# A Fourier-mixing and snake-MLP kernel: relayouts of the first batch on VectorE, filter halves by DMA, weight scaling on GpSimd, and the short chunk moved to the border of two batches

## The chip, the cores and the metric

The kernel runs on one core of a Trainium2 chip. The metric is the device time of one execution in microseconds (us), taken over several executions. On this core one run costs about 815 us and repeated runs mostly agree within a few us, so differences under about 0.3% are read only from several rounds. A change counts as faster or slower from 2% on; everything less is "the same".

The engines are TensorE (PE in the profile; PEld is its weight load), VectorE (DVE), ScalarE (ACT), GpSimd (POOL) and SyncE (SP, which here only issues transfers; SPq is its sequencer).

## The reference, cut to what matters

```python
X = np.fft.rfft(x, axis=1)                 # x: 8 batches x 3008 x 256
y = np.fft.irfft(X * (filt_r + 1j * filt_i)[None], n=3008, axis=1)
h = y.reshape(24064, 256) @ w_in           # 256 -> 2048
g = h + np.sin(alpha * h) ** 2 / alpha
out = g @ w_out                            # 2048 -> 256
```

## The kernel before

The Fourier transform of 3008 = 47 x 64 points is done as matmuls with tables, in four stages for each batch: first (tile `pa`), forward (`pb`), a product with the filter (`p`), inverse (`pc`), last (`pd`, which gives `y`). Between first and forward, and again between inverse and last, data must move from one layout over the partitions to another. Before, that is a round trip through DRAM: a write to `d`, then a read with another address pattern (`t`).

```python
def first(self, i):
    ...
    if j == 3:
        nc.sync.dma_start(out=self.d1_rows[:, 8 * ch:8 * ch + 8, :], in_=self.t1)
def load_t2(self, g):                       # the way back, in the other layout
    for p in range(2):
        marks["t2", g] = eng.dma_start(out=self.t2[g][64 * p:64 * p + 64, :, :],
                                       in_=self.d1[a0:a0 + 6, :, :].rearrange("s n c -> n s c"))
```

A complex product needs the filter in both partition halves. For the first `FUSED = 2` batches each unit has two products and two inverse matmuls; from then on it is *fused*: the spectrum is swapped between the halves by a small DMA (`xs`), and two more VectorE instructions (`cross`) let one inverse matmul do.

```python
def dup_filter(g):                          # VectorE fills the other halves, with a sign
    for ins in (nc.vector.tensor_copy(out=f_t[0][64:128, gs, :], in_=f_t[0][0:64, gs, :]),
                nc.vector.tensor_scalar(out=f_t[1][0:64, gs, :], in0=f_t[1][64:128, gs, :],
                                        scalar1=-1.0, scalar2=None, op0=ALU.mult)):
        behind(ins, marks["prod", 3 * g - 2] if g else s1_dve)
...
def weights_out(i):                         # w_out / alpha, in steps 4 to 7
    for jb in range(4 * i, 4 * i + 4):
        nc.vector.tensor_scalar(out=w2[:, jb, :], in0=w_out32[:, jb, :], scalar1=rec_t[:, jb:jb + 1],
                                scalar2=-0.5, op0=ALU.mult, op1=ALU.mult)
```

The MLP runs over chunks of 512 tokens in eight steps each: two hidden tiles (matmul `ph`, a sine on ScalarE into `cos`, the snake on VectorE into `v`) and, for the chunk before, projection matmuls (`po`). The Fourier stages of the next batch are put between these steps by hand: `put(step, function, ...)`.

```python
chunks = [(pb, c0, min(512, 2 * S - c0)) for pb in range(B // 2) for c0 in range(0, 2 * S, 512)]
```

A pair of batches has 6016 tokens, eleven chunks of 512 and one of 384, which stands at the end.

## Time and profile before

The median is 815.4 us (815.29 to 816.07); the profiled execution took 814.22 us with a span of 812.3 us.

| Mark in the trace | us |
|---|---|
| first forward matmul | 27.03 |
| first hidden-layer matmul (`ph`) | 53.46 |
| first projection matmul (`po`) | 69.18 |
| from there to the end of the span | 743.1 |

Two marks cut such a kernel well. Up to the first `ph` it is a start-up chain of dependent steps; between the first `ph` and the first `po` it fills the first chunk; after that TensorE has work all the time. So "when does `po` start" and "how long is the rest" are two numbers to compare between versions.

The page's busy tenths in 40 slices (20.3 us each), before. The third row, PEclk, is the granted TensorE clock in tenths.

```profile
PE   5657999999999999999999999999999999999995
DVE  3669797789978998789987998779987999777772
PEclk9779999999999999999999999999999999999998
```

TensorE is loosely busy only in the first four slices. The windows view, before (length, then busy time and instruction count of each engine, granted clock, DMA share, GB/s):

```profile
90.00:180.00 90.00, 89.67 (x669) 62.35 (x667) 72.11 (x129) 71.95 (x142) 11.04 (x19) 1.00 0.59 144
180.00:300.00 120.00, 118.46 (x892) 82.36 (x890) 106.21 (x202) 97.67 (x196) 8.51 (x15) 1.00 0.60 135
300.00:800.00 500.00, 498.76 (x3716) 345.93 (x3714) 415.68 (x742) 391.58 (x770) 27.46 (x44) 1.00 0.47 113
```

From 90 us on TensorE (the first figure after the length) idles 3.1 us in 710. There is little to win there but fewer matmuls or those last microseconds. The timeline of TensorE, before (start, length, what ran; in brackets the idle time before it and what ended it):

```profile
27.03 1.01 PE L179 MATMUL pb<-t,d_t 128*128 128x256 f16 x4 [4.88 <-DMA t<-d]
...
51.38 0.81 PE L230 MATMUL pd<-wi_t,t 96*128 96x94 f16 x8 [8.56 <-DMA t<-d]
...
53.46 1.87 PE L368 MATMUL ph<-y,w 128*128 128x512 f16 x4 [0.17 <-ACT y L136]
...
69.18 1.04 PE L383 MATMUL po<-w,v 128*128 128x256 f16 x8
```

Both relayouts show as a wait for a DMA: 4.88 and 8.56 us. And the VectorE work that the change will touch, from VectorE's timeline before: a filter copy with a sign, and four scalings of `w_out`.

```profile
30.32 0.56 DVE L275 TENSOR_SCALAR filt<-filt 64x1536 f16<-64x1536 f16 x1
...
62.58 1.13 DVE L351 TENSOR_SCALAR w<-w_out,rec_t 128x256 f16<-128x256 f32 x4
```

Each scaling took 0.33 to 0.35 us.

### The profile page before, as it was taken

What the parts mean: (1) busy time and instruction counts of PE and PEld (TensorE: products, weight loads), DVE (VectorE), ACT (ScalarE), POOL (GpSimd) and SP (SyncE); (2) the same over time, 40 slices, a digit from 0 to 9 for tenths busy, and PEclk for the clock granted to TensorE, in tenths of its full rate; (3) what the DMA queues carried; (4) which work ended last, traced back from release to release, by engine and by line L of the source; (5) the groups of instructions that cost most, each with busy time, mean ns of one, the idle gap of its engine ahead of it and who ended that gap; (6) DMA issues with size and microseconds to landing.
All of it is one profiled execution on the core that took longest, in us unless ns stands there. A gap on an engine that the chain in (4) does not pass through costs nothing.

```text
span 812.3 us, 16130 instructions
## 1 busy us (share of the span) xinstructions
PE 771.4 (95%) x5649; PEld 527.5 (65%) x5649; DVE 652.4 (80%) x1191; ACT 612.8 (75%) x1200; POOL 65.4 (8%) x111
## 2 busy tenths in 40 slices
PE   5657999999999999999999999999999999999995
PEld 2324676676666776667667676667667676666674
DVE  3669797789978998789987998779987999777772
ACT  4547787788878888778887887778887887777662
POOL 3210300110020000200002000200002000000000
PEclk9779999999999999999999999999999999999998
DMA  9985755466576465644657554654558333411111
GB/s 213 227 260 132 186 113 148 127 137 141 117 185 149 97 144 126 184 95 95 140 159 178 111 104 116 193 127 104 115 139 214 73 91 84 116 37 40 40 40 46
DMA packets 86201, 104.44 MB, mean 129 GB/s; under 512 B 10388, under 2 KB 72868, under 8 KB 86120
## 3 DMA queue, kind: packets, MB, share of 16 engines
q1 hardware_dynamic: 73904, 73.45, 34.3%
q0 software_dynamic: 10288, 29.11, 18.0%
q10 hardware_dynamic: 1928, 0.86, 0.4%
q8 instruction: 44, 0.72, 0.4%
q14 instruction: 37, 0.30, 0.1%
HBM read 58.02 MB, written 49.81 MB: 133 GB/s over the span
## 4 chain that ended last, share of the span: by engine, by line
PE 88%; DMA 5%; DVE 2%; ACT 2%; issue 1%; POOL 0%; SPq 0%; ACTq 0%; DVEq 0%; POOLq 0%
PE po L383 39%; PE ph L368 38%; PE pa L159 4%; PE pc L210 3%; PE pb L179 3%; PE pd L230 2%; DMA t<-d 2%; DMA x<-in_x_dram 2%; DVE v L372 1%; ACT cos L371 1%; DMA d<-t 1%; ACT t L136 1%; DVE p L193 1%; DMA d<-g 0%; DVE t L138 0%
## 5 line engine op out<-in xcount | busy, mean ns | idle before, releaser
L372 DVE SCALAR_TENSOR_TENSOR v<-cos,ph 128x512 f16<-128x512 f32 (+1 forms) x768 | 483.5, 672 | 119.3 <-ACT cos L371 116.2
L371 ACT ACTIVATE cos<-ph 128x512 f32<-128x512 f32 (+1 forms) x768 | 411.5, 591 | 99.7 <-PE ph L368 98.9
L368 PE MATMUL ph<-y,w 128*128 128x512 f16 (+1 forms) x1536 | 388.5, 375 | 0.8 <-DVE y L138 0.6
L383 PE MATMUL po<-w,v 128*128 128x256 f16 x3008 | 389.0, 272 | 0.0
L383 PEld LDWEIGHTS <-v 128*128 128x128 f16 x3008 | 289.2, 98 | 77.7 <-issue 1.7
L368 PEld LDWEIGHTS <-w 128*128 128x128 f16 x1536 | 148.1, 98 | 104.3 <-issue 3.6
L182 ACT CAST xf<-pb 128x512 f16<-128x512 f32 x96 | 56.9, 594 | 20.4 <-PE pb L179 17.3
L389 ACT COPY o<-po 128x512 f32<-128x512 f32 x96 | 55.6, 579 | 17.9 <-PE po L383 16.3
L136 ACT CAST t<-pa 96x512 f16<-96x512 f32 x88 | 51.2, 585 | 22.8 <-PE pa L159 22.6
L159 PE MATMUL pa<-x,wf_t 94*96 94x512 f16 x128 | 51.0, 408 | 11.7 <-DMA x<-in_x_dram 8.3
L230 PEld LDWEIGHTS <-t 96*128 96x128 f16 x512 | 36.1, 99 | 34.3 <-DMA t<-d 11.0
L170 POOL DMA_DIRECT2D t<-d x56 | 37.0, 676 | 251.1 <-PE ph L368 183.6
L230 PE MATMUL pd<-wi_t,t 96*128 96x94 f16 x512 | 43.0, 208 | 11.5 <-DMA t<-d 10.1
L193 DVE TENSOR_TENSOR p<-xf,filt 128x512 f16<-128x512 f16 x120 | 47.8, 418 | 6.3 <-ACT xf L182 6.1
L136 ACT CAST y<-pd 128x376 f16<-128x376 f32 x82 | 39.3, 480 | 17.0 <-PE pd L230 16.6
L136 ACT CAST g<-pc 128x512 f16<-128x512 f32 x65 | 38.4, 590 | 11.8 <-PE pc L210 11.6
L210 PE MATMUL pc<-p,e_t 128*128 128x256 f16 x240 | 44.0, 278 | 2.7 <-DVE p L193 1.5
L179 PE MATMUL pb<-t,d_t 128*128 128x256 f16 x192 | 38.2, 282 | 5.9 <-DMA t<-d 4.9
L118 POOL DMA_DIRECT2D x<-in_x_dram x32 | 17.0, 536 | 262.8 <-PE pc L210 145.9
L138 DVE CAST t<-pa 96x512 f16<-96x512 f32 x40 | 27.2, 680 | 12.6 <-PE pa L159 12.6
L210 PEld LDWEIGHTS <-e_t 128*128 128x128 f16 x240 | 23.0, 99 | 16.2 <-issue 2.5
L200 DVE TENSOR_TENSOR p<-p,xs 128x512 f16<-128x512 f16 x72 | 30.6, 425 | 2.5
(31 smaller groups left out, 155.2 us busy)
## 6 DMA issues: line engine op xcount, KB each, us to landing
d<-t SPq DMA_DIRECT2D x32, 384.0 KB
d<-g SPq DMA_DIRECT2D x64, 192.0 KB
t<-d SPq DMA_DIRECT2D x32, 384.0 KB
x<-in_x_dram POOLq DMA_DIRECT2D x32, 376.0 KB, 6.2
t<-d POOLq DMA_DIRECT2D x56, 192.0 KB, 7.0
xs<-xf SPq DMA_DIRECT2D x144, 64.0 KB
out_dram<-o SPq DMA_DIRECT2D x72, 94.0 KB
w_in<-in_moe_w_in_dram POOLq DMA_DIRECT2D x2, 1024.0 KB, 8.9
```

What stands on the lines that cost most here:

```text
L136: marks["act"] = nc.scalar.copy(out=dst, in_=src)
L159: marks["pe"] = nc.tensor.matmul(out=ps[0:NK, :], lhsT=wf_t, rhs=self.x[ch][:, 2 * j:2 * j + 2, :], start=True, stop=True)
L179: nc.tensor.matmul(out=ps[:, i, :], lhsT=d_t[:, s, :], rhs=self.t2[s // 6][:, s % 6, :], start=True, stop=True)
L182: nc.scalar.copy(out=self.xf[u], in_=ps)
L193: marks["prod", u] = nc.vector.tensor_tensor(out=pt, in0=self.xf[u], in1=f_t[k][:, 2 * u:2 * u + 2, :], op=ALU.mult)
L210: nc.tensor.matmul(out=ps[:, i, :], lhsT=e_t[:, k, 2 * w + i, :], rhs=pt[:, i, :], start=(k == 0), stop=(k == len(pr) - 1))
L230: nc.tensor.matmul(out=psv[:, i, :], lhsT=self.t4[ch][:, 4 * half + i, cb * 128:cb * 128 + 128], rhs=wi_t, start=True, stop=True)
L368: nc.tensor.matmul(out=ps[:, 0:n], lhsT=w1[:, cb, jb * 128:jb * 128 + 128], rhs=y_cols[:, cb, c0:c0 + n], start=(cb == 0), stop=(cb == 1))
L371: nc.scalar.activation(out=cs[:, 0:n], in_=ps[:, 0:n], func=AFT.Sin, bias=float(np.pi / 2))
L372: marks["snake"] = nc.vector.scalar_tensor_tensor(out=v[k][:, jb, 0:n], in0=cs[:, 0:n], scalar=-1.0, in1=ps[:, 0:n], op0=ALU.add, op1=ALU. ...
L383: nc.tensor.matmul(out=pso[k][:, t % 2, :], lhsT=v[k][:, jb, 128 * t:128 * t + 128], rhs=w2[:, jb, :], start=(jb == 0), stop=(jb == 15))
L389: nc.scalar.copy(out=o[:, 0:nb, :], in_=pso[k][:, 0:nb, :])
```

## The change

The intent is to shorten the start-up chain. Batch 0 no longer goes through DRAM: VectorE transposes 32x32 blocks of 32-bit pairs in place of each round trip. The filter halves are copied by DMA, now without the sign, so batch 0 takes the sign from a second inverse table. GpSimd, which in the kernel before ran only four memsets of 0.1 us and the issue of transfers, scales `w_in` and half of `w_out`. Later batches need the negated filter half, so GpSimd flips its sign in place (`negate`), and batch 1 is fused like the rest (`FUSED = 1`). The 384-token chunk moves to the border of the two batches of a pair.

```diff
-FUSED = 2
+FUSED = 1
...
+    for g in range(2):                     # filter halves by DMA, no sign
+        for k in range(2):
+            gs = slice(12 * g, 12 * g + 12)
+            nc.gpsimd.dma_start(out=f_t[k][64 - 64 * k:128 - 64 * k, gs, :],
+                                in_=f_t[k][64 * k:64 * k + 64, gs, :])
...
+    def turn(dst, src):
+        nc.vector.transpose(out=dst.bitcast(UINT32).rearrange("p s c k -> p c (s k)"),
+                            in_=src.bitcast(UINT32).rearrange("p s c k -> p c (s k)"))
+    def turn_back(i):
+        hc, cs = i // 2, slice(32 * (i % 2), 32 * (i % 2) + 32)
+        turn(t4_0[hc][:, :, cs], g_0[hc][:, :, cs])
...
+    for i in range(4):
+        turn(t2_0[i // 2][:, :, 32 * (i % 2):32 * (i % 2) + 32], t1_0[:, :, 32 * i:32 * i + 32])
...
+        ins = nc.gpsimd.tensor_tensor(out=w1[:, :, js], in0=w32, in1=cos_cols[...], op=ALU.mult)
...
+    nc.vector.reciprocal(out=rec, in_=al)  # now just before the hidden layer
...
-            nc.vector.tensor_scalar(
+            (nc.gpsimd if jb in range(8, 16) else nc.vector).tensor_scalar(
                 out=w2[:, jb, :], in0=w_out32[:, jb, :], scalar1=rec_t[:, jb:jb + 1],
                 scalar2=-0.5, op0=ALU.mult, op1=ALU.mult)
...
-    chunks = [(pb, c0, min(512, 2 * S - c0)) for pb in range(B // 2) for c0 in range(0, 2 * S, 512)]
+    chunks = [(pb, c0, 384 if c0 == 2560 else 512) for pb in range(B // 2)
+              for c0 in [*range(0, 2561, 512), *range(2944, 2 * S, 512)]]
...
+    def negate(i):
+        gs = slice(6 * i, 6 * i + 6)
+        nc.gpsimd.tensor_scalar(out=f_t[1][0:64, gs, :], in0=f_t[1][0:64, gs, :],
+                                scalar1=-1.0, scalar2=None, op0=ALU.mult)
+    for i in range(4):
+        put(9, negate, i)
...
-        z = 48 * b - 2 * (b % 2)
+        z = 48 * b - 0 * (b % 2)
...
-            inv = 22.5 + u if b == 1 else ...
-            fwd = inv - (1.5 if b == 1 else 6)
+            inv = 23 + 1.3 * u if b == 1 else ...
+            fwd = inv - (5 if b == 1 else 6)
```

The cuts hold the new tables, eight filler matmuls before the hidden layer (`warm_pe`, meant for TensorE's clock), the order of the loads, and the block loop of batch 0 (twelve blocks of forward, product and inverse).

## The prediction

> **What bounds it now.** Two regimes. From 100 to 800 us the windows view gives TensorE 696.9 busy of 700 us: dense, so only fewer matmuls help there. Before that stands a start-up chain: the timeline has the first hidden-layer matmul at 53.46 us, and the chain of waits shows why. First-stage matmuls end at 16.9; the DRAM relayout follows (write 4.9 us, read back 4.3 us; first forward matmul at 27.0); products and inverse matmuls run to 43.4 (VectorE 9.7 of 10 us busy at 30-40, including filter copies of 0.57 and 0.56 us); then the second relayout (3.2 + 3.8 us) to 51.4. After it, the first chunk is VectorE-bound (13.8 of 15.7 us busy); the first projection matmul starts at 69.2. DMA is at or over 0.8 of its engines for most of the first 69 us.
>
> **Removed.** Both DRAM round trips of batch 0 (26.9-17.5 = 9.4 us, and 51.4-43.4 = 8 us), VectorE's eight filter copies (4.5 us), weight scaling on VectorE (4.9 us) and half of the 5.5 us of output-weight scaling. Batch 1 becomes fused: 24 matmuls fewer at 0.109 us = 2.6 us.
>
> **Added.** Eight block transposes of 1024 32-bit elements. [...] of which four stand on the chain in front and about two behind. Filters must be loaded whole and copied by DMA before the products: from the 205 to 270 GB/s of the first 20 us I estimate both halves of the filter landed at 19.5 us, the first copies at 23.5, the second at 29. So products wait for the copies[...]. ScalarE then evacuates both sides, 2 x 0.59 us per block of twelve. GpSimd scales w1[...].
>
> **Stages after the change (estimates).** Products from 23; inverse ends 37-38; two transposes; first hidden matmul at 41 (36 to 46) rather than 53.5. The first chunk takes VectorE 2.5 us less: first projection at 55-57 rather than 69.2, unless w_out (after alpha on a full DMA queue, estimated landing 45-54 us) holds VectorE. From there TensorE's work is dense and 2 us shorter. Batch 1, now three products per unit at one unit per 1.3 steps, loads VectorE 8.9, 10.3, 11.2 and 9.1 us in four consecutive half chunks in which TensorE has 8.5 to 8.7: I subtract 3 us for that. Sum: about -12.5 -2 +3, and a margin of 2 lost to weights or the clock's recovery: nearly all of it from the critical start-up chain. The 384-token chunk only moves a deadline.
>
> **Predicted: 802 us, 794 to 811 in 8 of 10 cases.** Faster by over 2% (below 799.1) 0.30; within 2% 0.68; slower 0.02.
>
> **What would show it.** First forward matmul near 19-20 us, first product near 23 and released by a filter-copy DMA; [...] first hidden matmul near 41; [...] TensorE idle 2-4 us more than before in the stretch of batch 1's products, released by VectorE; 24 fewer 256-column inverse matmuls per run in the dense part.
>
> **What would make it wrong.** Filter copies much faster or slower than 250 GB/s; strided transposes at twice my estimate; GpSimd's weights slowed by VectorE and pacing the first chunk (slower by up to 5 us); w_out late; or batch 1's VectorE load not costing TensorE anything (then near 798, just faster).

"My estimate" in the last paragraph is the time of a transpose. The time of two transposes is inside the 41 us, and so inside the 12.5 us; it is the author's estimate. The sum as written is 815.4 − 12.5 − 2 + 3 = 803.9 us, with the margin of 2 it is 805.9, and 802 was put down. "The clock's recovery" is about the granted clock, which in the kernel before was 0.60 from 20 to 30 us, 0.70 from 50 to 60 and 1.00 from 60 to 70.

## The result, and the profile after

The changed kernel took 823.3 us (median of 4 runs, 820.88 to 824.38) against 815.35 (4 runs, 815.29 to 816.07). The ratio is 1.009, with a 95% interval from 1.0067 to 1.0116: "the same" by the 2% rule, but above the predicted range of 794 to 811. Ratios here are the mean time of one kernel's fast runs over the mean of the other's fast runs of the same rounds, so they are not quite the ratio of the medians.

The profiled execution took 824.38 us, span 822.6 us. Busy tenths after:

```profile
PE   5774989999999999999999999999999999999995
DVE  6788669779987899789987899789987899777772
PEclk9976999999999999999999999999999999999999
```

The start is denser than before, but the fourth slice (62 to 82 us) has TensorE at 4 tenths and the clock at 6. TensorE's timeline, after:

```profile
20.30 1.06 PE L339 MATMUL pb<-t_h,d_t 128*128 128x128 f16 x8
...
45.18 6.26 PE L453 MATMUL ph<-y,w 128*128 128x512 f16 x16
...
73.53 1.87 PE L453 MATMUL ph<-y,w 128*128 128x512 f16 x4 [12.68 <-DVE v L457]
...
75.62 1.91 PE L468 MATMUL po<-w,v 128*128 128x256 f16 x8
```

The first hidden matmul is 8.3 us earlier than before, as intended. Then one hidden tile waits 12.68 us for a snake on VectorE, and the first projection comes 6.4 us *later* than before. VectorE's timeline, after, has the reason for the wait in its last lines:

```profile
14.19 3.63 DVE L310 STREAM_TRANSPOSE t_h<-t 128x1024 uint32<-128x1024 uint32 x2 [0.38 <-ACT t L149]
17.68 2.31 DVE L310 STREAM_TRANSPOSE t<-t 128x1024 uint32<-128x1024 uint32 x2
...
25.18 4.28 DVE L349 TENSOR_TENSOR p<-xf,filt 128x512 f16<-128x512 f16 x11 [1.30 <-DMA filt<-filt]
...
35.29 7.26 DVE L310 STREAM_TRANSPOSE t_h<-t_h 128x1024 uint32<-128x1024 uint32 x4
...
43.96 0.93 DVE L426 RECIPROCAL rec<-al 16x128 f32<-16x128 f32 x1
...
54.60 1.95 DVE L435 TENSOR_SCALAR w<-w_out,rec_t 128x256 f16<-128x256 f32 x4
...
58.12 14.77 DVE L435 TENSOR_SCALAR w<-w_out,rec_t 128x256 f16<-128x256 f32 x4
```

The same four scalings that took 1.13 us before take 14.77 us. VectorE counts as busy all that time, so a table of busy shares does not give it away; the length of the instruction does. The view of this one source line, after, gives the count and the shortest, median and longest of them in ns:

```profile
L435 DVE TENSOR_SCALAR w<-w_out,rec_t x8: 498/1546/4161, 54.6 to 68.7; 128x256 f16<-128x256 f32 x8
```

And GpSimd's timeline, after:

```profile
38.66 9.58 POOL L389 TENSOR_TENSOR w<-w_in,cos_all 128x768 f16<-128x768 f32 x6
52.65 3.75 POOL L435 TENSOR_SCALAR w<-w_out,rec_t 128x256 f16<-128x256 f32 x8 [4.42 <-DMA w_out<-in_moe_w_out_dram]
56.38 16.36 POOL L505 TENSOR_SCALAR filt<-filt 64x1536 f16<-64x1536 f16 x4
```

The longest scaling took 4.16 us, and beside it GpSimd ran four sign flips of 4.09 us each, from 56.38 to 72.74 us. VectorE's 14.77 us end at 72.89. One scaling per flip fits both: taken singly, the four took 2.53 us (it began while the first flip ran) and then 4.16 us three times. Also note the line at 54.60: these four scalings took 1.95 us instead of 1.13, and beside them GpSimd ran scalings of 0.47 us each.

Last, the windows after:

```profile
60.00:75.00 15.00, 1.85 (x5) 0.69 (x5) 15.00 (x8) 0.84 (x2) 12.74 (x4) 0.64 0.00 0
90.00:180.00 90.00, 83.89 (x610) 56.49 (x609) 70.83 (x135) 67.83 (x136) 13.12 (x21) 0.98 0.62 156
180.00:300.00 120.00, 119.87 (x901) 83.11 (x898) 105.17 (x194) 97.94 (x192) 8.24 (x14) 1.00 0.55 129
300.00:800.00 500.00, 499.89 (x3725) 346.37 (x3723) 421.28 (x756) 395.63 (x780) 27.73 (x46) 1.00 0.47 115
```

Three things are seen. From 60 to 75 us TensorE has 1.85 us of work and its clock falls to 0.64. From 90 to 180 us, the stage of batch 1, it idles 6.1 us, where before it idled 0.3. From 180 us on it is denser than before: 0.2 us idle in 620 after, 2.8 before.

So the span grew by 10.3 us as follows: first hidden matmul 8.3 us earlier, first chunk 14.7 us longer (30.4 instead of 15.7 us), the rest 3.9 us longer (747.0 instead of 743.1).

### Theories

*Lock.* The flips on GpSimd hold something that VectorE's scalings need, so each scaling waits out a whole flip. What that something is, no trace here shows. Its rival: the scalings wait for the late `w_out` or for the queue of work, and the flips only run beside them.

*Fused batch 1.* Fusing it costs more than its 24 saved matmuls give. Within it are two rivals for the cause: VectorE's three products per unit are too much (the prediction), or the swaps `xs` come late.

*Start-up* (S). What keeps the hidden layer at 45 instead of 41 us are the late reciprocal and the four last transposes standing one behind the other.

### The profile page after: what moved, and what is told of

The parts are those of the page before. It is cut to its first block, busy times and chain, and to the rows that moved or that the text cites. A ratio compares the mean times of both kernels' runs of the same rounds, so it can differ in the third digit from the quotient of the medians.

```text
span 822.6 us, 16328 instructions
## 1 busy us (share of the span) xinstructions
PE 774.6 (94%) x5745; PEld 530.3 (64%) x5745; DVE 672.1 (82%) x1184; ACT 616.1 (75%) x1203; POOL 89.9 (11%) x122
## 4 chain that ended last, share of the span: by engine, by line
PE 81%; DVE 8%; DMA 6%; ACT 2%; issue 1%; POOL 1%; ACTq 0%; POOLq 0%
PE po L468 37%; PE ph L453 36%; DVE v L457 3%; PE pa L170 3%; PE pd L247 2%; PE pb L190 2%; DVE w L435 2%; PE pc L221 2%; DMA xs<-xf 2%; DMA filt<-in_filt_i_dram 2%; DMA t<-d 1%; DVE t_h L310 1%; DMA filt<-filt 1%; ACT t_h L149 1%; DMA d<-t_h 1%
## 5 line engine op out<-in xcount | busy, mean ns | idle before, releaser
L457 DVE SCALAR_TENSOR_TENSOR v<-cos_all,ph 128x512 f16<-128x512 f32 (+1 forms) x768 | 483.0, 672 | 109.8 <-ACT cos_all L456 106.4
L456 ACT ACTIVATE cos_all<-ph 128x512 f32<-128x512 f32 (+1 forms) x768 | 411.4, 591 | 114.3 <-PE ph L453 111.7
L453 PE MATMUL ph<-y,w 128*128 128x512 f16 (+1 forms) x1536 | 390.7, 378 | 12.8 <-DVE v L457 12.7
L193 ACT CAST xf<-pb 128x512 f16<-128x512 f32 x84 | 49.9, 594 | 18.5 <-PE pb L190 13.8
L149 ACT CAST t_h<-pa 96x512 f16<-96x512 f32 x77 | 45.1, 586 | 10.9 <-PE pa L170 10.7
L247 PEld LDWEIGHTS <-t_h 96*128 96x128 f16 (+1 forms) x512 | 35.9, 98 | 26.9 <-DVE t_h L310 4.6
L247 PE MATMUL pd<-wi_t,t_h 96*128 96x94 f16 (+1 forms) x512 | 42.5, 206 | 4.6 <-DVE t_h L310 3.5
L170 PE MATMUL pa<-x,wf_t 94*96 94x512 f16 x112 | 43.0, 386 | 2.2 <-ACT t_h L149 2.1
L210 DVE TENSOR_TENSOR xs<-xs,filt 128x512 f16<-128x512 f16 x84 | 35.1, 418 | 6.1 <-DMA xs<-xf 6.0
L204 DVE TENSOR_TENSOR p<-xf,filt 128x512 f16<-128x512 f16 x84 | 35.1, 418 | 2.0 <-ACT xf L193 2.0
L221 PE MATMUL pc<-p,e_t 128*128 128x256 f16 x168 | 32.1, 273 | 3.7 <-ACT y L149 2.8
L151 DVE CAST y<-pd 128x376 f16<-128x376 f32 x49 | 26.6, 543 | 0.6 <-PE pd L247 0.6
```

The source lines that it names most:

```text
L149: marks["act"] = nc.scalar.copy(out=dst, in_=src)
L170: marks["pe"] = nc.tensor.matmul(out=ps[0:NK, :], lhsT=wf_t, rhs=self.x[ch][:, 2 * j:2 * j + 2, :], start=True, stop=True)
L193: nc.scalar.copy(out=self.xf[u], in_=ps)
L221: nc.tensor.matmul(out=ps[:, i, :], lhsT=e_t[:, 2 * w + i, :], rhs=pt[:, i, :], start=(k == 0), stop=(k == len(pr) - 1))
L247: nc.tensor.matmul(out=psv[:, i, :], lhsT=lhsT, rhs=wi_t if self.b else wi0_t, start=True, stop=True)
L453: nc.tensor.matmul(out=ps[:, 0:n], lhsT=w1[:, cb, jb * 128:jb * 128 + 128], rhs=y_cols[:, cb, c0:c0 + n], start=(cb == 0), stop=(cb == 1))
```

## The experiments

Eleven kernels ran in three calls, each call on one chip beside the kernel before (medians of before: 814.51, 814.81 and 814.76 us). Except for e3, all gave right results. By the 2% rule each of them is "the same" as the kernel before. The columns ph and po are the starts of the first hidden and first projection matmul in the run's profile, "rest" is the span less po.

| Run | us, median (range) | ratio to before [95%] | ph | po | rest |
|---|---|---|---|---|---|
| before | 815.4 | 1 | 53.46 | 69.18 | 743.1 |
| after | 823.3 | 1.0091 [1.0067, 1.0116] | 45.18 | 75.62 | 747.0 |
| e1 flips after the scalings | 809.52 (808.12–811.44) | 0.9935 [0.9909, 0.9961] | 45.27 | 60.62 | 745.8 |
| e2 scalings on ScalarE | 812.82 (812.60–813.56) | 0.9977 [0.9956, 0.9998] | 44.92 | 62.71 | 748.1 |
| e3 two flips of four | 817.18 (815.97–817.72) | 1.0025 [1.0006, 1.0045] | 45.81 | 69.12 | 746.7 |
| e4 batch 1 unfused | 817.00 (815.73–817.95) | 1.0024 [1.0003, 1.0045] | 46.35 | 61.07 | 753.6 |
| e5 the same, short distance | 803.10 (802.17–806.48) | 0.9846 [0.9820, 0.9872] | 47.73 | 64.63 | 740.1 |
| e6 e1, x of batch 2 later | 807.07 (804.30–807.64) | 0.9892 [0.9866, 0.9918] | 45.52 | 62.42 | 742.5 |
| e7 e1, start-up reordered | 809.72 (808.60–810.95) | 0.9932 [0.9909, 0.9954] | 46.15 | 62.14 | 745.4 |
| e8 e1, swaps from ScalarE | 815.68 (814.53–817.40) | 1.0006 [0.9982, 1.0030] | 45.65 | 62.51 | 753.1 |
| e9 e5, reciprocal early | 802.64 (802.44–805.27) | 0.9858 [0.9845, 0.9871] | 43.68 | 60.49 | 740.3 |
| e10 e5, chunks as before | 807.91 (806.64–811.04) | 0.9923 [0.9908, 0.9938] | 45.44 | 61.11 | 743.8 |
| e11 e5, filter copies on VectorE | 804.63 (803.23–805.04) | 0.9870 [0.9856, 0.9884] | 45.87 | 63.06 | 740.0 |

The profiled execution of e5 was the slowest of its four (806.48 us), with a clock of 0.71 from 45 to 60 us, so its ph and po are late; its rest is what to read. The clock in that stretch differs between the other profiles too: 1.00 in e1, e4, e7 and e9, 0.97 in e2, 0.77 to 0.89 in after, e3, e6, e8, e10 and e11. e6 has e1's start unchanged, yet its first chunk took 16.9 us against 15.4 at 0.78, so a difference of 1 to 2 us in po can be the clock's and not the edit's.

### e1: the flips wait for the scalings

Nothing is removed. The flips only get a dependency on VectorE's last scaling.

```diff
+            if jb == 7:
+                marks["w_out_dve"] = ins
...
+        after(ins, marks["w_out_dve"])     # on each of the four flips
```

> Edit: the four GpSimd sign flips of the filter wait for the last output-weight scaling on VectorE; nothing else changes. Theory L ([...] each VectorE scaling that reads and writes SBUF waits out one 4.1 us GpSimd flip, which started first): the four scalings take about 0.35-0.5 us each instead of 14.8 us together, TensorE's wait of 12.7 us in the first chunk goes, time about 810 (808-812). Rival D (VectorE waits for the output weights' DMA or is slow by itself): the scalings stay slow, time 821-824. Rival G (GpSimd is simply late and the whole start waits for it): the stall only moves to a later wait, time 818-824.

It took 809.5 us, 13.8 us less than the changed kernel. VectorE's timeline, e1:

```profile
53.66 1.82 DVE L435 TENSOR_SCALAR w<-w_out,rec_t 128x256 f16<-128x256 f32 x4
...
57.05 1.13 DVE L435 TENSOR_SCALAR w<-w_out,rec_t 128x256 f16<-128x256 f32 x4
```

GpSimd's timeline, e1:

```profile
58.27 16.27 POOL L507 TENSOR_SCALAR filt<-filt 64x1536 f16<-64x1536 f16 x4 [1.53 <-DVE w L435]
```

The four scalings are back at 1.13 us, and the 12.7 us wait is gone. The flips take their 4.07 us as before, so it was not VectorE that made them long. And while they ran, from 56 to 76 us, twenty snakes on VectorE averaged 0.679 us, against 0.683 for the same shape in the kernel before. The snake has one input in PSUM, and these instructions were not held at all. The scaling, which was held, has one source tile and goes from SBUF to SBUF. Why the one was held and the other not, the trace does not show.

### e2: the scalings on ScalarE

```diff
-            (nc.gpsimd if jb in range(8, 16) else nc.vector).tensor_scalar(...)
+            if jb in range(8, 16): nc.gpsimd.tensor_scalar(...)
+            else: nc.scalar.mul(w2[:, jb, :], w_out32[:, jb, :], rec_h[:, jb:jb + 1])
```

> Edit: the eight VectorE scalings of the output weights are done by ScalarE instead; the GpSimd sign flips stay where they are, at the same time. Theory L: [...] its scalings take about 0.3-0.4 us each beside the flips, and the flips keep about 4.1 us each; time 808-812. Rival D: the ScalarE scalings wait for the same DMA, so the stall stays, 820-824. Rival G: stall stays as well.

It took 812.8 us. The flips begin at 55.86 us, as early as in the changed kernel. ScalarE's last four scalings, from 56.01 on and beside a flip, took 1.74 us together; its first four, before any flip, 1.72. The 12.7 us wait is gone with the flips left where they were. It is 3.3 us slower than e1: ScalarE has 3.5 us more to do in the first chunk, which took 17.8 us against 15.4; that the one comes of the other was not tested, and the rest is 2.3 us longer, with a granted clock of 0.77 from 62.7 to 70 us. So data and timing of `w_out` were not to blame: on ScalarE the same scalings run beside the same flips.

### e3: two flips instead of four (a wrong result on purpose)

```diff
-    for i in range(4):
+    for i in range(2):
         put(9, negate, i)
```

> Edit: only two of the four GpSimd sign flips are issued (a wrong result on purpose: half of the filter keeps its sign for batches 1 to 7). Theory L: two of the last four VectorE scalings are blocked for about 4 us each, the other two take about 0.35 us; stall halves to about 6 us; time 815-818. Rivals D and G without a lock: D unchanged 821-824; G also 815-818, so this run alone only sizes the dose.

Half of the flipped half keeps the wrong sign, so the result is wrong (relative error 0.67). VectorE's timeline, e3:

```profile
57.90 8.49 DVE L435 TENSOR_SCALAR w<-w_out,rec_t 128x256 f16<-128x256 f32 x4
```

Half the flips give about half the loss: 8.49 us (the first of the flips began at 57.55), and 6.1 us off the time of the changed kernel. With e1 and e2 this shows that the flips hold up the scalings: the loss follows the number of flips, goes away if they come after, and goes away if the scalings are done elsewhere. Through what they hold them up, no run here shows.

### e4 and e5: batch 1 unfused

Batch 1 takes two products and two inverse matmuls again. For this the second table must outlive batch 0, so it is put into the half of `y` that batch 1 fills later, and the flips move to step 44, behind batch 1's products. e4 keeps the distances of the changed schedule, e5 takes those of the kernel before.

```diff
-FUSED = 1
+FUSED = 2
-    e1_0 = by_half(t4_h[1])
+    e1_v = [y[:, i, 1]...[:, 0:2048] for i in range(2)]      # e4 and e5
-        put(9, negate, i)
+        put(44, negate, i)                                  # after batch 1's last product
-            inv = 23 + 1.3 * u if b == 1 else ...
-            fwd = inv - (5 if b == 1 else 6)
+            inv = 22.5 + u if b == 1 else ...                # e5 only
+            fwd = inv - (1.5 if b == 1 else 6)               # e5 only
```

> Edit: batch 1 goes back to two products and two inverse matmuls (no swap by DMA), its second table kept in the half of y that is still empty; the sign flips move behind batch 1's products (step 44). So the stall of the first chunk goes too: compare with e1_negate_late. Theory F (the fused form costs batch 1 about 6 us of TensorE idle in 90-180 us, through late swaps on the busy DMA queue, for 2.6 us of matmuls saved): about 3-4 us below e1, so about 806-807. Rival (the idle comes from the late reads of the relayout and the next batch's x loads on the DMA queue, not from the swaps): equal to e1 or 2.6 us slower, 810-813.

e4 was badly made and tells nothing of fusing. With forward five steps ahead of inverse, the four buffers of `p` hold only two units of two products, and VectorE stands waiting: it was busy for 11.79 us from 90 to 110 us and 12.17 from 110 to 130, against 17.60 and 17.04 in e5. The time was 817.0 us, the rest at 753.6 us.

> The first unfused run left forward and inverse 5 steps apart, so its four product buffers held only two units and VectorE waited for them; this one takes the distances of the kernel before (inverse at 22.5 + u, forward 1.5 steps ahead). To compare with e1_negate_late (809.5). Theory F (the fused form of batch 1 costs TensorE about 6 us of idle through swaps that come late): TensorE's idle between 75 and 180 us falls from 6.9 to 1-3 us, 24 more matmuls cost 2.6 us, time 805-808. Rival (the idle is caused by the relayout reads and x loads alone): idle stays at 5-7 us, time 810-813.

e5 took 803.1 us: 6.4 us less than e1, and 1.5% less than the kernel before. TensorE's idle time between 75 and 180 us fell from 6.9 to 1.0 us. The windows of e1, the kernel to compare with:

```profile
90.00:110.00 20.00, 15.77 (x118) 10.44 (x116) 14.57 (x32) 13.47 (x27) 0.52 (x1) 1.00 0.46 100
110.00:130.00 20.00, 19.57 (x134) 12.80 (x133) 19.76 (x41) 15.97 (x31) 0.52 (x1) 1.00 0.62 144
```

The same windows of e5:

```profile
90.00:110.00 20.00, 20.00 (x158) 14.60 (x157) 17.60 (x36) 16.59 (x34) 0.52 (x1) 1.00 0.57 120
110.00:130.00 20.00, 20.00 (x147) 14.17 (x145) 17.04 (x33) 16.03 (x33) 8.93 (x4) 1.00 0.51 111
```

Unfused, TensorE is full. Fused, it idles 4.2 us from 90 to 110. In the first half of that VectorE has only 4.67 of 10 us of work: it was waiting, not overloaded. After it VectorE is full (29.7 us of work from 100 to 130), and TensorE loses 1.2 us there; how much of this is a delay being made up, and how much the load of three products, was not separated. But from 75 to 180 us VectorE had 85.3 us of work in e5, where TensorE hardly idled, and 84.6 in e1. What VectorE waited for is seen in the changed kernel. The waits view from 85 to 135 us (us in total, times, longest):

```profile
DVE xs L210 <- DMA xs<-xf: 5.7, 2, 4.0
```

The longest of these waits in VectorE's timeline of the same kernel:

```profile
110.53 0.43 DVE L210 TENSOR_TENSOR xs<-xs,filt 128x512 f16<-128x512 f16 x1 [3.96 <-DMA xs<-xf]
```

SyncE's timeline, which holds what it issued:

```profile
100.56 1.18 SPq L197 DMA_DIRECT2D xs<-xf  x2
102.30 5.91 SPq L486 DMA_DIRECT2D out_dram<-o  x5
108.31 3.47 SPq L197 DMA_DIRECT2D xs<-xf  x4
```

VectorE waited 5.7 us for swaps, and between two swaps SyncE spent 5.91 us issuing five stores of the output, one of them 4.5 us long. The DMA engines were full then (the windows view has a DMA share of 1.03 from 100 to 103 us, and 0.78 from 103 to 108). The order matters: the 4.0 us wait was for the first swap (two transfers), which was issued at 100.56 us, *before* those stores, and was not used until 110.53. The second swap was issued only after them, at 108.31; the wait for it was 1.7 us. So the stores in the same queue can have held the second swap, but they do not explain the longer wait. Whether it is the queue or the full DMA engines, e6 and e8 were to tell.

### e6: batch 2's loads of x later

```diff
-                put((12,18,25,32)[ch] if b == 2 else ..., s.load_x, ch)
+                put((24,27,30,33)[ch] if b == 2 else ..., s.load_x, ch)    # on top of e1
```

> Edit on e1_negate_late: batch 2's x loads move from steps 12, 18, 25, 32 to 24, 27, 30, 33, so that batch 1's relayout reads have the DMA engines to themselves. Theory Q (the swaps sit behind an output store on the Sync queue whose issue is held up 3.9 us because the engines are full with relayout reads and x): most of the 3.8 us wait of VectorE for the first swap goes, TensorE idle at 90-100 us falls from 3.45 to 1-2.5 us, time 807-808.5. Rival (relayout reads alone fill the engines): unchanged 809-810.

It took 807.1 us, 2.4 us less than e1, with intervals that just overlap. TensorE's work from 90 to 110 us rises from 15.77 to 19.70 us, but from 110 to 130 it falls from 19.57 to 18.23. VectorE's waits for swaps fall from 5.3 us to 2.3, and TensorE's idle time between 75 and 180 us from 6.9 to 3.9. This points to the collision with these loads as part of the loss, of which some only moves.

### e8: the swaps issued from ScalarE's queue

```diff
-                    nc.sync.dma_start(out=self.xs[u][...], in_=self.xf[u][...])
+                    (nc.scalar if b == 1 else nc.sync).dma_start(...)      # on top of e1
```

> Edit on e1_negate_late: batch 1's 24 swaps are issued from ScalarE's DMA queue instead of the Sync queue, so no output store stands ahead of them; sizes and engines are the same. Theory Q: [...] VectorE's wait for swaps falls from 5.3 to under 2 us, TensorE idle in 75-110 us falls by 3 us or more, time 805.5-807.5 unless ScalarE's issue time (0.5 us each) costs as much. Rival (the transfer itself is slow on full engines): wait stays about 4-5 us, time 809-811.

It took 815.7 us, 6.2 us more than e1. Issuing a pair of swaps cost ScalarE 1.1 to 1.3 us (0.56 to 0.66 each), and by the trace ScalarE then also waited for VectorE's products (5.5 us in two waits, 4.2 of them in one), which free the swap buffers. VectorE's waits for swaps did fall to 1.7 us, as theory Q expected, but VectorE came to the first swap later (97.04 us, against 94.42 in e1), so by its time this run is inconclusive. Its trace says more. The first swap was issued at 86.68 us, with no store in its queue, and was still not used until 97.04, about 10 us later, as in e1 (84.62 to 94.42) and in the changed kernel. The DMA queues of e8 from 87 to 91 us (packets, MB, share of the 16 engines), where q10 holds the swaps and q0 what GpSimd issued, the relayout reads and the loads of `x`:

```profile
q0 software_dynamic: 233, 0.77, 98.1%
q10 hardware_dynamic: 8, 0.01, 0.7%
```

So for the first swap the traces point to the full DMA engines (98.1% for q0 alone), not to the stores; how much of the 6.4 us this makes, no run separates.

### e7: a reordered start-up

On top of e1 the reciprocal moves to the front, and the blocks are ordered so that the first half of batch 0 is done earlier and its two transposes stand between products.

```diff
-    blocks = [(hc, w) for w0 in (0, 3) for hc in range(2) for w in range(w0, w0 + 3)]
+    blocks = [(0, 0), (0, 1), (0, 2), (1, 0), (1, 1), (0, 3), (0, 4), (0, 5), (1, 2), (1, 3), (1, 4), (1, 5)]
-        if i - 3 == 8 + 2:
-            turn_back(0); turn_back(1)
+        if i in (10, 11):
+            turn_back(i - 10)
```

> Edit on e1_negate_late, in the start only: the reciprocal of alpha and its transpose come early instead of just ahead of the first hidden matmul, and the blocks of batch 0 are ordered so that the first channel half is complete after block 8 of 12 and its two transposes back run between products. Theory S (the start missed its estimate by four transposes back of 1.9 us on the chain [...], and 1.5 us for the reciprocal): first hidden matmul at 40-42 us instead of 45.2, time 805.5-807. Rival (weights from GpSimd or DMA hold the first hidden matmul anyway, or the first chunk absorbs it): hidden matmul at 44-45 or time 808-810.

It took 809.7 us, as e1. VectorE's timeline, e7:

```profile
35.20 2.00 DVE L313 STREAM_TRANSPOSE t_h<-t_h 128x1024 uint32<-128x1024 uint32 x1 [0.53 <-ACT t_h L149]
37.06 0.73 DVE L355 TENSOR_TENSOR p<-xf,filt 128x512 f16<-128x512 f16 x2
37.70 1.91 DVE L313 STREAM_TRANSPOSE t_h<-t_h 128x1024 uint32<-128x1024 uint32 x1
```

The first two transposes now stand between products, but there they hold up the products of the last blocks, which the last two transposes wait for. The first hidden matmul stands at 46.15 us, 0.9 later than in e1. VectorE is itself the chain there, and putting its work in another order took nothing off it.

### e9: e5 with the reciprocal early

```diff
+    nc.vector.reciprocal(out=rec, in_=al)      # now beside the first memsets; its transpose
+    ...                                        # and copy before the block loop
```

> Edit on e5_unfused_short (803.1): only the reciprocal of alpha, its transpose and its copy come early. TensorE waited 1.5 us for them just ahead of the first hidden matmul. Theory S: first hidden matmul at 43.5-44 us, time 801-802.5. Rival (the matmul then waits for GpSimd's first weights or the activation copy instead): 802.5-804.

It took 802.6 us, 0.5 us less than e5 by the medians, which their intervals do not separate. In the profile the first hidden matmul is at 43.68 us, against 45.27 in e1 with the same clock: the reciprocal's 1.5 us are seen, if not in the total. This is the best profile.

### e10: e5 with the chunks of the kernel before

```diff
-    chunks = [(pb, c0, 384 if c0 == 2560 else 512) ...]
+    chunks = [(pb, c0, min(512, 2 * S - c0)) for pb in range(B // 2) for c0 in range(0, 2 * S, 512)]
-        z = 48 * b - 0 * (b % 2)
+        z = 48 * b - 2 * (b % 2)               # and the other offsets of odd batches
```

> Edit on e5_unfused_short: the 384-token chunk goes back to the end of each pair of batches, with the offsets of the kernel before, so that odd batches are needed 2 to 4 steps earlier. Theory C (in the dense part the chunk only moves a deadline that was met already; the kernel before idles 1.5 us at 180-300 and 1.2 us at 300-800, the changed one 0.1 and 0.1): 0.5-3 us slower, 803.5-806. Rival (it is worth nothing, or odd batches now come late and idle appears in every pair): within 0.5 us, or above 807.

It took 807.9 us, 4.8 us more than e5. The rest is 743.8 us, within 0.7 us of the kernel before, against 740.1 in e5. Windows of e10:

```profile
110.00:130.00 20.00, 18.00 (x130) 12.26 (x129) 14.58 (x27) 14.46 (x29) 12.45 (x4) 1.00 0.59 136
130.00:150.00 20.00, 19.40 (x143) 12.83 (x142) 14.88 (x24) 16.46 (x33) 4.35 (x2) 1.00 0.44 131
```

TensorE loses 2.6 us here that e5 does not lose, and 2.0 of them are one wait of a last-stage matmul for the data read back from DRAM. With the long chunk, batch 1 has to be ready two to four steps earlier. From 180 to 790 us e10 idles 2.1 us and e5 0.2. So the border chunk removes real waits.

### e11: e5 with the filter copied by VectorE

```diff
-            nc.gpsimd.dma_start(out=f_t[k][64 - 64 * k:128 - 64 * k, gs, :], in_=...)
+            nc.vector.tensor_copy(out=f_t[k][64 - 64 * k:128 - 64 * k, gs, :], in_=...)   # two before the loop, two in it
```

> Edit on e5_unfused_short: the other halves of the filter are copied by VectorE again (four copies of 64 x 3072, estimated 1.1 us each from the 0.57 us of 64 x 1536), not by DMA. Theory P (products wait for the filter-copy DMA until 25.2 us and the copies load the DMA queue by 1.6 MB): first pair of products complete at 22.5-23.5, w_out and weights land earlier, first hidden matmul 1-2 us earlier, time 801-802.5. Rival (ScalarE's table scalings until 25.5 us and its evacuations hold the start, so nothing is gained, or VectorE's copies delay it): 803-805.

It took 804.6 us; the interval overlaps that of e5. VectorE's timeline, e11:

```profile
20.10 1.94 DVE L282 COPY filt<-filt 64x3072 f16<-64x3072 f16 x2
22.37 1.43 DVE L358 TENSOR_TENSOR p<-xf,filt 128x512 f16<-128x512 f16 x4 [0.33 <-ACT xf L351]
26.36 1.43 DVE L358 TENSOR_TENSOR p<-xf,filt 128x512 f16<-128x512 f16 x4 [2.56 <-ACT xf L351]
```

The products start at 22.37 with both halves there, where the changed kernel waited for a copy until 25.18. But the next products wait 2.56 us for ScalarE (in the changed kernel it works on three tables from 22.40 to 25.55 us; its timeline in e11 was not read), and the hidden layer begins no sooner (45.87 us). The copies by DMA are neither the limit nor a gain that can be measured.

## Why the prediction was wrong

One path leads from the kernel before to the changed one in four steps, by medians. The first and the third change several things at once:

| Step | us | difference |
|---|---|---|
| before → e10: the new start-up, batch 1 unfused, old chunks | 814.8 → 807.9 | −6.9 |
| e10 → e5: 384-token chunk at the border | 807.9 → 803.1 | −4.8 |
| e5 → e1: batch 1 fused, with its schedule; flips earlier, but after the scalings | 803.1 → 809.5 | +6.4 |
| e1 → after: the flips not held back | 809.5 → 823.3 | +13.8 |

The steps add up by construction; what they show is the size of each part. They mix runs in which the kernel before moved by 0.3 us.

**The step that failed: "The first chunk takes VectorE 2.5 us less: first projection at 55-57".** The first chunk took 30.4 us instead of the 14 to 16 that this means. The count of VectorE's work was right (half of the `w_out` scalings did leave), and with the flips held back (e1) the chunk took 15.4 us, as predicted. But the flips of `negate` were never sized. They are named nowhere in the prediction. The only interference between the two engines that it names is GpSimd's weights "slowed by VectorE"; what happened is the reverse: the flips took 4.10 us beside the scalings and 4.08 in e1, the scalings up to 4.16 instead of 0.34. Two readings of the change were missed. First, `put(9, ...)` fixes the flips' place in GpSimd's own order, but it does not hold them until step 9: nothing else was there for GpSimd to do, so they started the moment its scalings ended, at 56.38 us. Second, it was not asked whether VectorE's remaining scalings run freely beside 16.4 us of flips. They do not, as e1, e2 and e3 show. The trace of the kernel before could not tell, since GpSimd did no such work in it.

**"Products from 23; inverse ends 37-38; two transposes; first hidden matmul at 41": right in kind, too small.** Forward at 20.30 (19 to 20 predicted); products complete from 25.18, released by a filter copy (23 predicted); inverse ends at 36.1 (37 to 38). Then *four* transposes of 1.9 us stand on the chain, 7.26 us, of which 6.5 lie behind the last inverse matmul, where the prediction had two. The two transposes with a contiguous destination took 1.19 us for 128x1024 of 32 bits; the six with a strided destination took 1.87 to 1.95 us. The prediction named "strided transposes at twice my estimate" as a risk and did not put it into the sum. The reciprocal between the last stage and the hidden layer added 1.5 us. Hidden layer: 45.18.

**"I subtract 3 us for that" (VectorE's load in batch 1): the size was too small and the cause was another.** TensorE idled 5.8 us more than before from 90 to 180 us, and undoing the fusion gave 6.4 us. The longest single wait of TensorE there, 2.8 us, ended when VectorE had got its first swap (it waited 5.7 us for swaps in all); another 1.4 us was a forward matmul waiting for the relayout's read. The 24 saved matmuls, 2.6 us by the prediction's estimate, are within these 6.4 us, net. For the first swap e8's trace points to full DMA engines; for the others the cause of the delay stays open.

**"The 384-token chunk only moves a deadline": wrong in the other direction.** It is worth 4.8 us in e5, since that deadline was being missed.

**Right by luck:** that the time stays within 2% of before, the likeliest class. The forecast was 1.6% faster, and what was measured is 0.9% slower.

**Right:** `w_out` was not the cause (it had landed at 52.65 us); TensorE stays dense later. The GpSimd scalings of `w_in` took 1.83 us (median). The terms written in the prediction add up to 804 to 806 us, according to whether its margin is counted, so the 802 it put down was also on the hopeful side of its own sum. By the marks the error is 4 us in the hidden layer's start, some 15 us in the first chunk and about 3 us after it.

e5 and e9 beat both kernels: 802.6 to 803.1 us, 1.4 to 1.5% faster than before, and 2.5% by the medians faster than the change as it was given.

## What to carry to other kernels

Before moving work to an idle engine, list what the busy engines do at that very time and find out by a run whether the two hold each other up. Here VectorE's scalings of `w_out`, from SBUF to SBUF, took 0.34 us with GpSimd idle (e1) and up to 4.16 us beside one of its flips (the changed kernel). Not every instruction is held: the snakes, with an input in PSUM, took 0.68 us either way, and two transposes ran beside GpSimd's scalings of `w_in` (from 38.66 us) at 1.95 and 1.94 us, against 1.94 and 1.89 for the two ahead of them. A place in a hand-made schedule orders one engine's work but does not delay it (the flips, put at step 9, began at 56.38 us, as GpSimd's scalings ended): if it must not run early, give it a dependency. When an instruction in the trace is many times longer than its twin elsewhere, the engine may count as busy but be waiting (VectorE was busy for 15.00 of 15 us from 60 to 75 us); compare the shortest and the longest of a group (498 and 4161 ns), not busy shares.

## What the runs measured of the hardware

- A block transpose of 128x1024 of 32 bits on VectorE took 1.19 us with a contiguous destination and 1.87 to 1.95 us with a strided one, a step of 256 bytes here (the changed kernel).
- The fp16 multiply by a constant on 64x1536 took GpSimd 4.10 us in the changed kernel and 4.08 in e1, where it held up no scaling; VectorE did the same shape in 0.56 us in the kernel before.
- A VectorE scaling that takes 0.34 us with GpSimd idle (e1) took about 0.5 us beside GpSimd's scalings (four in 1.95 us) and up to 4.16 us beside such a flip, one whole flip. Four flips that were not held back cost 13.8 us (e1's median against that of the changed kernel).
- With the DMA engines full, one store held SyncE for 4.5 us (the changed kernel, from 103.70 us; DMA share 1.03 from 100 to 103 us and 0.78 from 103 to 108), and in e8 a swap with no store in its queue took about 10 us from its issue to its use (GpSimd's queue at 98.1% from 87 to 91 us).
- The granted clock was 0.64 from 60 to 75 us, where TensorE had 1.85 us of work, 0.71 from 75 to 80 and 1.00 from 80 to 90; from 110 to 130, after a wait of TensorE of 2.8 us, it was 0.91. What this costs after the first projection is small by one profile each: a rest of 747.0 us against 745.8 in e1.
